# Top-32 attention into an ELU feed-forward: thresholds of both rows in one operation, and every second gate on GpSimd in the first nine blocks

## The chip, the core and the metric

The kernel runs on one core of a Trainium2 chip. The core has five engines, each with its own instruction queue worked in order: TensorE (PE in the profile, its weight loads PEld), VectorE (DVE), ScalarE (ACT), GpSimd (POOL) and SyncE (SP), which here only issues DMAs. The metric is device time in microseconds (us) of one execution, the median over several.

## The reference

Two stages follow each other. The first is attention in which each query keeps only its 32 largest scores; the second is a feed-forward layer with an ELU between its two matrices.

```python
# q, k, v: (8, 8, 576, 64)
scores = scale * np.matmul(q, k.transpose(0, 1, 3, 2))
kth = np.partition(scores, -32, axis=-1)[..., -32:-31]
scores = np.where(scores >= kth, scores, -1000000000.0)
scores = scores - np.max(scores, axis=-1, keepdims=True)
attn = np.exp(scores)
attn = attn / (np.sum(attn, axis=-1, keepdims=True) + 1e-09)
x = np.matmul(attn, v)               # then (B, H, S, D) -> (B*S, H*D) = (4608, 512)
h = x @ w_in                         # w_in (512, 2048)
g = np.where(h > 0.0, h, np.exp(np.minimum(h, 0.0)) - 1.0)
out = g @ w_out                      # w_out (2048, 512)
```

The two weight matrices arrive as 64-bit floats and are turned into 32-bit floats on the chip.

## The kernel before

**Attention in steps.** The work is cut into 144 steps. A step is one tile of 128 queries and one pair of heads, so two rows of scores (i = 0 and 1) of 576 columns each. Its stations are spread over later steps of the main loop. In iteration n:

- `scores` computes the scores of step n+2 (PE, then a copy by ScalarE).
- `select` finds the 32nd largest value in both rows of step n on VectorE: four MAX8, each giving the next eight values, with three MATCH_REPLACE8 between them that blank what was found. The first eight values go to `u.first`, the last eight to `u.last`. `select` is a generator that stops four times, which cuts the iteration into quarters.
- `mask` (step n-1) turns the scores into masked exponentials, in place. With `low` the 32nd largest and `top` the largest value, GpSimd computes `neg = -low` (L368) and `gap = low - top` (L370) on 128x1 tiles, and ScalarE computes a Prelu with bias `neg` and a huge negative slope (L371), then an Exp with bias `gap` that also sums its row into `den` (L372). Row 0 is masked in the second quarter, row 1 in the third.
- `normalise` (step n-1) inverts the sums on GpSimd (L382 to L387, small operations) and scales both rows (L389, 128x576). It comes ahead of the last quarter's feed.
- `turn` (step n-2) transposes the weights on PE (L408) and copies them by ScalarE (L409); `attend` multiplies them with v (L434) and ScalarE copies the result into the block's `xT` (L461).

The first eight iterations (`n < tight`) have a loop of their own, in which the instructions' order is left to the compiler's scheduler and the weights are decoded (`hook`: L170 to L172 on ScalarE, L173 on GpSimd, L180 and L183 on VectorE, L187 on GpSimd). From the ninth on, the order on PE, ScalarE, VectorE and GpSimd is the order in which the program writes the instructions.

**Feed-forward in blocks.** Tokens are gathered in 19 blocks of one, two or three slots of 128 tokens. Blocks 0 to 4 have one slot, blocks 5 to 8 two, and then each group of four blocks has 2, 2, 3 and 2. A block has 16 `hidden` pieces and four `project` pieces for each slot. `feed`, called at each quarter of an iteration, issues as many pieces as its plan says are due.

A `hidden(f)` piece multiplies `xT` by a column strip of `w_in` on PE (L502, two PSUM buffers). ScalarE then writes the negative part into a scratch tile `n` (L510) and the positive part into `gT` (L511). After each second piece it takes the exponential of both `n` at once (L513); the scratch tile has two buffers, so it is written again two pairs later. `project` multiplies `gT` by `w_out` (L523) and sends the result out.

**The gates.** What is left of the ELU, `gT = gT + (n - 1)`, is the gate: one operation on VectorE for each pair of `hidden` pieces, eight for each block, over 256, 512 or 768 columns (L478). A pair puts its gate into the list `gates` with the quarter in which it was issued; `close_gates`, called by `feed` with keep = 2, issues those that are two quarters old, and `hidden` and `project` force out those that they need.

Of the kernel before, what the change touches and what calls it, by code (L numbers as in the profile page):

```python
# [8 lines left out]
AF = mybir.ActivationFunctionType  # L9
ALU = mybir.AluOpType  # L10
FP32 = mybir.dt.float32
# [12 lines left out]
class Tile:  # L24
# [6 lines left out]
    def __init__(self, b, qt, rows, block, cols):  # L31
        self.b, self.qt, self.rem = b, qt, qt == 4
        self.rows = rows
        self.block = block
        self.cols = cols
        self.ql = cols.stop - cols.start
# [21 lines left out]
class Step:  # L58
# [7 lines left out]
    def __init__(self, t, hp, group, at):  # L66
        self.t, self.hp = t, hp
        self.group, self.at = group, at
        self.masked = self.normal = self.turned = False
        if t.rem:  # L70
            rows = [(4 * hp, 0), (4 * hp + 2, 0), (4 * hp + 3, 1), (4 * hp + 1, 1)]
            self.heads = [
                (h, i, slice(64 * (n % 2), 64 * (n % 2) + 64))
                for n, (h, i) in enumerate(rows)
            ]
        else:
            self.heads = [(2 * hp + i, i, slice(0, 128)) for i in range(2)]
# [3 lines left out]
def kernel(  # L81
# [9 lines left out]
    nc = tc.nc  # L91
    P = nc.NUM_PARTITIONS
# [16 lines left out]
    def pool(name, bufs, **kw):  # L109
        return ctx.enter_context(tc.tile_pool(name=name, bufs=bufs, **kw))  # L110
# [7 lines left out]
    small = pool("small", 4)  # L118
# [75 lines left out]
    def hook():  # L194

        if not decode:
            return
        decode.pop(0)()
        if not decode:
            raws.close()  # L200
            late["f"] = ctx.enter_context(tc.tile_pool(name="f", bufs=2))
            late["g"] = ctx.enter_context(tc.tile_pool(name="g", bufs=2))
            late["x"] = ctx.enter_context(tc.tile_pool(name="xt", bufs=2))
# [79 lines left out]
    def turn_qk(whole=False):  # L283
        while turning:
            if next(turning[0], turning) is turning:
                turning.pop(0)
            elif not whole:
                return
# [3 lines left out]
    def scores(u):  # L292

        u.sc = scpool.tile([P, 2, S], FP32, tag="sc", name="sc")
        q0 = QUERIES + u.t.qt * P
        for half in range(2):
            for h, i, rows in u.heads:
                kq = kqT[u.t.b, h // 2]
                part = slice(i * D, (i + 1) * D)
                k0 = (KEYS if i == 0 else 0) + half * HS  # L300
                nc.tensor.matmul(  # L301
                    wide[i][rows, half, 0:HS],
                    kq[part, q0 : q0 + u.t.ql],
                    kq[part, k0 : k0 + HS],
                    start=True,
                    stop=True,
                )
        for i in range(2):
            nc.scalar.activation(  # L309
                u.sc[:, i, :].rearrange("p (a s) -> p a s", a=2),  # L310
                wide[i][:, :, 0:HS], AF.Copy, scale=scale,
            )

    def select_row(u, i):
        if i == 0:
            u.first = small.tile([P, 2, 8], FP32, tag="m1", name="m1")
            u.last = small.tile([P, 2, 8], FP32, tag="m4", name="m4")
        sc = u.sc[:, i, :]
        m = u.first[:, i, :]
        nc.vector.max(m, sc)  # L320
        wk = wkpool.tile([P, S], FP32, tag=f"wk{i}", name="wk")
        cur = sc
        for r in range(TOP_K // 8 - 1):
            nc.vector.match_replace(wk[:], m, cur, TAKEN)
            cur = wk[:]
            if r < TOP_K // 8 - 2:
                m = small.tile([P, 8], FP32, tag=f"m{i}", name="m")[:]
            else:
                m = u.last[:, i, :]
            nc.vector.max(m, cur)  # L330
            if r == 2 or u.t.qt > 0:
                hook()
            if r != 1:
                yield

    def select(u):

        u.first = small.tile([P, 2, 8], FP32, tag="m1", name="m1")
        u.last = small.tile([P, 2, 8], FP32, tag="m4", name="m4")
        cur = [u.sc[:, i, :] for i in range(2)]  # L340
        found = [u.first[:, i, :] for i in range(2)]
        for i in range(2):
            nc.vector.max(found[i], cur[i])  # L343
        yield
        wk = [wkpool.tile([P, S], FP32, tag=f"wk{i}", name="wk")[:] for i in range(2)]
        for r in range(TOP_K // 8 - 1):
            for i in range(2):
                nc.vector.match_replace(wk[i], found[i], cur[i], TAKEN)  # L348
            cur = wk
            for i in range(2):  # L350
                if r < TOP_K // 8 - 2:
                    found[i] = small.tile([P, 8], FP32, tag=f"m{i}", name="m")[:]
                else:
                    found[i] = u.last[:, i, :]
                nc.vector.max(found[i], cur[i])  # L355
            hook()
            yield

    def mask(u, i):

        if u.masked:
            return
        if i == 0:
            u.den = small.tile([P, 2], FP32, tag="den", name="den")
        u.masked = i == 1
        sc, low, top = u.sc[:, i, :], u.last[:, i, 7:8], u.first[:, i, 0:1]
        neg = small.tile([P, 1], FP32, tag="neg", name="neg")
        nc.gpsimd.tensor_scalar_mul(neg[:], low, -1.0)  # L368
        gap = small.tile([P, 1], FP32, tag="gap", name="gap")
        nc.gpsimd.tensor_tensor(gap[:], low, top, ALU.subtract)  # L370
        nc.scalar.activation(sc, sc, AF.Prelu, bias=neg[:], alpha=STEEP)  # L371
        nc.scalar.activation(  # L372
            sc, sc, AF.Exp, bias=gap[:], accum_out=u.den[:, i : i + 1]
        )

    def normalise(u):
# [92 lines left out]
    def close_gates(keep=0, upto=None):  # L469

        while gates:
            put, group, dst, n = gates[0]
            if put > place[0] - keep if upto is None else group > upto:
                return
            gates.pop(0)
            nc.vector.scalar_tensor_tensor(  # L478
                out=dst, in0=n, scalar=-1.0, in1=dst, op0=ALU.add, op1=ALU.add
            )  # L480
# [70 lines left out]
    blocks, tight = [], 2 * NHP  # L551
    for b in range(B):
# [12 lines left out]
        for qt in range(J + 1):  # L565
            r0 = b * S + (JP if qt == J else qt)
            if qt == J:
                (blk, slot), c0, n = slots[rest], (b % 2) * R, R
                rows = slice(r0, r0 + R)
            else:  # L570
                (blk, slot), c0, n = slots[(b % 2) * J + qt], 0, P
                rows = slice(r0, r0 + J * (P - 1) + 1, J)
# [8 lines left out]
        for qts in order:  # L581
            for hp in range(NHP // 2 if qts == (J,) else NHP):
                group = Group([tiles[qt] for qt in qts], hp)
                steps += [Step(tiles[qt], hp, group, i) for i, qt in enumerate(qts)]
            for qt in qts:
                n = len(steps)
# [59 lines left out]
    def step(n):  # L646
        return steps[n] if 0 <= n < NS else None
# [3 lines left out]
    for n in range(NS + 3):  # L651
        for fn, args in todo.pop(n, []):
            fn(*args)
        ahead, cur, prev, done = step(n + 2), step(n), step(n - 1), step(n - 2)
        if n < tight:
            turn_qk(True)
            scores(ahead)
            for i in range(2):
                passes = select_row(cur, i)
                next(passes)  # L660
                if i == 0:
                    while closing:
                        attend(closing.pop(0))
                elif prev:
                    normalise(prev)
                    turn(prev, main)
                    turn(prev, rest)
                    turn(prev, other)
                feed(n, 0.25)
                next(passes)  # L670
                mask(cur, i)
                feed(n, 0.25)
            continue
        if n == tight:
            ctx.enter_context(tc.manual_schedule(engines=engines))
        passes = select(cur) if cur else iter(range(4))
        if ahead:
            scores(ahead)
        while closing:
            attend(closing.pop(0))  # L680
        next(passes)
        feed(n, 0.25)
        if prev:
            mask(prev, 0)
        turn_qk()
        next(passes)
        feed(n, 0.25)
        if done:
            turn(done, main)
            turn(done, rest)  # L690
        if prev:
            mask(prev, 1)
        next(passes)
        feed(n, 0.25)
        if done:
            turn(done, other)
        next(passes)
        if prev:
            normalise(prev)
        feed(n, 0.25)  # L700
        turn_qk(True)
# [36 lines left out]
```

## Time and profile before

| | |
|---|---|
| median of 3 runs | 1682.49 us (1682.45 to 1682.61) |
| the profiled execution | 1682.55 us, span 1680.8 us |
| PE busy | 1604.5 us (95%) |
| VectorE busy | 1534.4 us (91%) |
| ScalarE busy | 1167.5 us (69%) |
| GpSimd busy | 638.8 us (38%) |
| gates on VectorE (L478) | 152, 106.5 us |
| thresholds on GpSimd (L368, L370) | 288 and 288, 73.5 and 61.1 us |

The span is the time between the first and the last instruction that the hardware profiler recorded in one execution; the execution's own time is 1.75 us longer. All busy times are from that execution. The busy time of PE counts the matmuls from start to modelled end, so a busy PE isn't PE at its peak. Matmul records can be missing by a few per cent.

### The profile page before, as it was taken

Reading aid. Unit: us, or ns where it says so; the run is one execution under the profiler, and the core shown is the slowest. Engines: PE = TensorE matmul, PEld = TensorE weight load, DVE = VectorE, ACT = ScalarE, POOL = GpSimd, SP = SyncE. Lnnn points to the kernel's source line nnn. Section 1 sums busy time; section 2 is a strip of 40 time slices with the busy share of each in tenths; the row PEclk is TensorE's granted clock in tenths of the full one; section 3 lists DMA queues with packets and bytes.
Section 4 is the critical chain, followed back from the end, with each engine's and each line's share of the span. In section 5 each row is a group of like instructions: output and inputs, shape, how many; then the busy total and the mean of one; then the engine's idle time right before and its main releaser. Section 6 shows DMA issues by size and latency. Waiting matters only on the chain.

```text
span 1680.8 us, 26396 instructions
## 1 busy us (share of the span) xinstructions
PE 1604.5 (95%) x8560; PEld 1041.7 (62%) x8560; DVE 1534.4 (91%) x3096; ACT 1167.5 (69%) x2661; POOL 638.8 (38%) x1719
## 2 busy tenths in 40 slices
PE   6767999999999999999999999999999999999999
PEld 4554776667575666656557575756558575755565
DVE  6999999999999999999999999999998999998600
ACT  6776786778776776767768685857758586857531
POOL 3776333433333334434334333333333333332200
PEclk8567999999999999999999999999999999999999
DMA  7441021001200111001200111001100000000000
GB/s 192 134 156 39 16 56 36 7 1 47 52 7 7 29 35 42 1 21 36 49 14 1 36 35 42 1 13 43 43 13 8 21 21 29 7 7 7 7 13 13
DMA packets 101129, 56.22 MB, mean 33 GB/s; under 512 B 84097, under 2 KB 92289, under 8 KB 100993
## 3 DMA queue, kind: packets, MB, share of 16 engines
q1 hardware_dynamic: 99792, 54.26, 11.6%
q8 instruction: 68, 1.11, 0.3%
q14 instruction: 69, 0.56, 0.1%
q10 hardware_dynamic: 1200, 0.30, 0.1%
HBM read 45.09 MB, written 9.44 MB: 32 GB/s over the span
## 4 chain that ended last, share of the span: by engine, by line
PE 59%; DVE 26%; ACT 5%; issue 1%; POOL 1%; ACTq 0%; DVEq 0%; POOLq 0%
PE ops L523 22%; PE hps L502 19%; DVE wk L348 11%; DVE m L355 9%; PE avps L434 7%; PE scps L301 6%; PE eps L408 4%; DVE m L343 3%; DVE gT L478 2%; ACT sc L372 1%; ACT sc L371 1%; PE qkps L271 1%; ACT et L409 1%; PE scps L408 1%; ACT n L510 0%
## 5 line engine op out<-in xcount | busy, mean ns | idle before, releaser
L502 PE MATMUL hps<-xT,w_in 128*128 128x256 f32 (+2 forms) x2432 | 557.4, 378 | 25.9 <-ACT gT L511 23.6
L355 DVE MAX8 m<-wk 128x8 f32<-128x576 f32 x816 | 574.5, 744 | 0.0
L523 PE MATMUL ops<-w_out,gT 128*128 128x512 f32 x1152 | 523.8, 599 | 0.0
L502 PEld LDWEIGHTS hps<-xT,w_in 128*128 128x128 f32 x2432 | 411.5, 195 | 127.4 <-ACT gT L511 34.4
L348 DVE MATCH_REPLACE8 wk<-m,wk 128x576 f32<-128x576 f32 x544 | 399.2, 740 | 0.0
L523 PEld LDWEIGHTS ops<-w_out,gT 128*128 128x128 f32 x1152 | 209.0, 190 | 233.6 <-issue 218.7
L382 POOL TENSOR_SCALAR dene<-den 128x2 f32<-128x2 f32 x144 | 34.8, 242 | 832.9 <-ACT sc L372 832.7
L371 ACT ACTIVATE sc<-sc,neg 128x576 f32<-128x576 f32 x288 | 226.4, 786 | 63.2 <-POOL neg L368 63.0
L372 ACT ACTIVATE sc<-sc,gap 128x576 f32<-128x576 f32 x288 | 223.2, 775 | 25.2
L309 ACT ACTIVATE sc<-scps 128x576 f32<-128x576 f32 x288 | 173.6, 662 | 76.6 <-PE scps L301 76.6
L389 POOL TENSOR_SCALAR sc<-sc,rec 128x576 f32<-128x576 f32 x288 | 219.5, 773 | 15.2 <-POOL rec L387 0.6
L409 ACT COPY et<-eps 128x512 f32<-128x512 f32 x288 | 167.5, 582 | 68.4 <-PE eps L408 68.2
L301 PE MATMUL scps<-kqT 64*128 64x288 f32 (+1 forms) x1280 | 200.5, 439 | 15.1 <-ACT kqT L277 8.3
L348 DVE MATCH_REPLACE8 wk<-m,sc 128x576 f32<-128x576 f32 x272 | 199.6, 740 | 0.0
L408 PEld LDWEIGHTS eps<-ident,sc 128*128 128x128 f32 x1152 | 145.1, 145 | 82.9 <-issue 48.0
L478 DVE SCALAR_TENSOR_TENSOR gT<-n,gT 128x512 f32<-128x512 f32 (+2 forms) x152 | 106.5, 701 | 97.7 <-ACT n L513 97.6
L434 PE MATMUL avps<-et,vT 128*64 128x256 f32 (+2 forms) x2080 | 190.4, 326 | 2.7 <-ACT et L409 2.3
L343 DVE MAX8 m<-sc 128x8 f32<-128x576 f32 x272 | 191.0, 742 | 0.0
L408 PE MATMUL eps<-ident,sc 128*128 128x128 f32 x1152 | 178.1, 281 | 12.9 <-POOL sc L389 11.9
L510 ACT ACTIVATE n<-hps 128x256 f32<-128x256 f32 (+2 forms) x304 | 112.6, 370 | 85.5 <-PE hps L502 75.0
L434 PEld LDWEIGHTS avps<-et,vT 128*64 128x64 f32 x2080 | 123.5, 141 | 73.1 <-issue 24.2
L301 PEld LDWEIGHTS scps<-kqT 64*128 64x128 f32 (+1 forms) x1280 | 107.7, 181 | 83.6 <-issue 44.8
(47 smaller groups left out, 1226.8 us busy)
## 6 DMA issues: line engine op xcount, KB each, us to landing
kin<-in_k_dram SPq DMA_DIRECT2D x64, 128.0 KB, 2.8
raw<-in_moe_w_in_dram SPq DMA_DIRECT2D x16, 512.0 KB, 4.4
vT<-in_v_dram SPq DMA_DIRECT2D x64, 128.0 KB, 2.3
raw<-in_moe_w_out_dram SPq DMA_DIRECT2D x16, 512.0 KB, 3.2
out_dram<-osb SPq DMA_DIRECT2D x32, 256.0 KB, 2.3
qin<-in_q_dram SPq DMA_DIRECT2D x62, 128.0 KB, 2.8
kin<-in_k_dram SPq DMA_DIRECT2D x32, 32.0 KB, 2.5
vT<-in_v_dram SPq DMA_DIRECT2D x64, 16.0 KB, 2.2
```

The costliest lines, as they stand in the source:

```text
L301: nc.tensor.matmul(wide[i][rows, half, 0:HS], kq[part, q0 : q0 + u.t.ql], kq[part, k0 : k0 + HS], start=True, stop=True,)
L343: nc.vector.max(found[i], cur[i])
L348: nc.vector.match_replace(wk[i], found[i], cur[i], TAKEN)
L355: nc.vector.max(found[i], cur[i])
L371: nc.scalar.activation(sc, sc, AF.Prelu, bias=neg[:], alpha=STEEP)
L372: nc.scalar.activation(sc, sc, AF.Exp, bias=gap[:], accum_out=u.den[:, i : i + 1])
L389: nc.gpsimd.tensor_scalar(u.sc[:, i, :], u.sc[:, i, :], rec[:, i : i + 1], 1.0, ALU.mult, ALU.mult)
L408: nc.tensor.transpose(ps[:, c * P : (c + 1) * P], sc[:, c0 : c0 + P], ident[:])
L409: nc.scalar.copy(g.et[:, chunks, u.at, :], ps[:, 0 : n * P].rearrange("p (c q) -> p c q", c=n),)
L434: nc.tensor.matmul(ps[i * D : (i + 1) * D, cols], vt[:, 2 * J + i if c == J else i * J + c, :], w, start=(c == 0), stop=(c == J),)
L502: nc.tensor.matmul(ps[:, 0:n_tok], w_in[:, i, f * P : (f + 1) * P], blk.xT[:, i, 0:n_tok], start=(i == 0), stop=(i == NC - 1),)
L523: nc.tensor.matmul(blk.o[:], blk.gT[f // NG][:, f % NG, s * P : (s + 1) * P], w_out[:, f, :], start=(f == 0), stop=(f == NF - 1),)
```

## The change

The diff does two things.

*Thresholds.* A new function `bounds` computes `neg` and `gap` for a range of rows on 128x2 tiles. From the ninth iteration on it is called once a step, for both rows, at the head of the iteration (behind that iteration's loads, ahead of `scores`), where before each row had its own pair of operations inside `mask`. In the first eight iterations it is called once for each row, right ahead of `mask`.

*Gates.* `close_gates` sends some gates to GpSimd: those of blocks 0 to 8 (the first half of 19, rounded down) whose first piece f has f % 4 == 2, which is every second gate. There the gate is two operations: `n = n - 1` in place, then `gT = gT + n`.

```diff
+    def bounds(u, rows):
+
+        if u.neg is None:
+            u.neg = small.tile([P, 2], FP32, tag="neg", name="neg")
+            u.gap = small.tile([P, 2], FP32, tag="gap", name="gap")
+            u.den = small.tile([P, 2], FP32, tag="den", name="den")
+        low, top = u.last[:, rows, 7], u.first[:, rows, 0]
+        nc.gpsimd.tensor_scalar_mul(u.neg[:, rows], low, -1.0)
+        nc.gpsimd.tensor_tensor(u.gap[:, rows], low, top, ALU.subtract)
+
     def mask(u, i):
 
         if u.masked:
             return
-        if i == 0:
-            u.den = small.tile([P, 2], FP32, tag="den", name="den")
         u.masked = i == 1
-        sc, low, top = u.sc[:, i, :], u.last[:, i, 7:8], u.first[:, i, 0:1]
-        neg = small.tile([P, 1], FP32, tag="neg", name="neg")
-        nc.gpsimd.tensor_scalar_mul(neg[:], low, -1.0)
-        gap = small.tile([P, 1], FP32, tag="gap", name="gap")
-        nc.gpsimd.tensor_tensor(gap[:], low, top, ALU.subtract)
+        sc, neg, gap = u.sc[:, i, :], u.neg[:, i : i + 1], u.gap[:, i : i + 1]
         nc.scalar.activation(sc, sc, AF.Prelu, bias=neg[:], alpha=STEEP)
         nc.scalar.activation(
-            sc, sc, AF.Exp, bias=gap[:], accum_out=u.den[:, i : i + 1]
+            sc, sc, AF.Exp, bias=gap, accum_out=u.den[:, i : i + 1]
         )
...
             gates.pop(0)
+            if group[0] < len(blocks) // 2 and group[1] % 4 == 2:
+                nc.gpsimd.tensor_scalar_add(n, n, -1.0)
+                nc.gpsimd.tensor_tensor(dst, dst, n, ALU.add)
+                continue
             nc.vector.scalar_tensor_tensor(
                 out=dst, in0=n, scalar=-1.0, in1=dst, op0=ALU.add, op1=ALU.add
             )
...
                 feed(n, 0.25)
                 next(passes)
+                bounds(cur, slice(i, i + 1))
                 mask(cur, i)
                 feed(n, 0.25)
             continue
         if n == tight:
             ctx.enter_context(tc.manual_schedule(engines=engines))
         passes = select(cur) if cur else iter(range(4))
+        if prev and prev.neg is None:
+            bounds(prev, slice(0, 2))
         if ahead:
             scores(ahead)
```

More of the change, by code (lines that the diff above doesn't have):

```diff
@@ L69, in __init__ @@
         self.masked = self.normal = self.turned = False
+        self.neg = None
         if t.rem:
```

## The prediction

> **What bounds the kernel now.** I read the page's busy slices first, then busy time by stretches of the span, then the chain of waits, then the waits of the engines that the change touches.
>
> ```profile
> PE 1604.5 (95%) x8560; PEld 1041.7 (62%) x8560; DVE 1534.4 (91%) x3096; ACT 1167.5 (69%) x2661; POOL 638.8 (38%) x1719
> ...
> 50.00:156.00 106.00, 77.19 (x357) 54.99 (x353) 100.21 (x174) 82.12 (x186) 76.33 (x108) 0.68 0.36 119
> 156.00:282.50 126.50, 113.42 (x880) 82.62 (x880) 125.68 (x263) 90.16 (x238) 47.08 (x137) 0.97 0.14 35
> 282.50:365.00 82.50, 76.62 (x559) 55.46 (x560) 81.90 (x176) 63.08 (x175) 32.78 (x97) 1.00 0.01 4
> 365.00:717.00 352.00, 346.87 (x1920) 232.60 (x1918) 351.34 (x720) 261.61 (x594) 137.57 (x397) 1.00 0.10 26
> 717.00:1590.00 873.00, 869.44 (x4423) 542.49 (x4422) 833.20 (x1685) 615.10 (x1353) 321.79 (x923) 1.00 0.08 22
> ```
>
> The first line is the whole span (busy time per engine). The others are stretches, with the busy time of PE, PEld, DVE, ACT and POOL in that order, then PE's granted clock, the DMA share and GB/s. Two engines are nearly full and hand over to each other. From 717 to 1590 PE has 3.6 us idle in 873, and DVE 40. From 365 to 717 DVE has 0.7 us idle and PE 5.1. Before 282 PE has holes and POOL is busiest while the weights are decoded (76 of 106 us).
>
> ```profile
> 282.77 0.31 ACT n L513
> 283.08 0.02 issue
> 283.10 0.42 DVE gT L478
> 283.53 1.46 DVE wk L348 x3
> ...
> 711.96 0.68 DVE m L355
> 712.98 0.78 ACT sc L371
> ...
> 717.59 2.37 PE avps L434 x18
> 719.96 3.63 PE ops L523 x8
> ```
>
> This is the chain of work that ended last (start, us, what). It says where a gate's time counts. At 283 it passes from ACT to DVE: a gate had to wait for its exponential. From there to 712 it runs almost only on DVE, gates included, and from 717 to the end it is PE. From 156 to 282 it alternates between PE and ACT, without DVE; at about 135 to 156 it is decode work on DVE and POOL. So DVE time removed between 283 and 717 can shorten the run, but only by as much as PE has slack there; DVE time removed elsewhere mostly becomes idle time.
>
> **The change: what leaves DVE.** Blocks 0 to 8 have eight gates each, and the second, fourth, sixth and eighth leave: 36 in all. By the gate's rows that is half of 5.51 us before 156, of 7.05 from 156 to 282, of 6.46 from 282 to 365, and of 22.60 from 365 to 717: 2.8, 3.5, 3.2 and 11.3, together 20.8 us.
>
> **What they cost on GpSimd.** No row shows this pair of operations. The one-input half is near L389 (0.75 us for 576 columns) and L386 (0.20 us for 2): 0.96 ns a column, so 0.44 us for 256 columns and 0.69 for 512. For the add, the nearest row is the integer add L187, 1.29 us for 512; with the 0.21 us of L385 for 2 columns that gives 0.75 for 256. A gate is then 1.19 us (twenty of 256 columns) or 1.98 us (sixteen of 512): 55.5 us of POOL. From below, an add as quick as a one-input pass makes it 38; from above, twice the integer row makes it about 91. I take 55.5, the row of the same shape. The thresholds give back POOL time: L368 and L370 cost 0.255 and 0.212 us, and from the ninth step on two of the four disappear, 136 x 0.47 = 64 us over the run.
>
> **Is POOL's part hidden?** POOL works in order, so the question is where the gates stand in its queue.
>
> ```profile
> POOL dene L382 <- ACT sc L372: 186.4, 34, 8.3
> POOL neg L368 <- DVE m L355: 8.9, 17, 1.7
> ```
>
> These are POOL's waits from 365 to 717 (us in total, times, longest). Once per step POOL sits 5.5 us waiting for ScalarE's exponential sum before it can normalise. From the steps of the two-slot blocks (5 to 8) on, the moved gates are closed in the first or second quarter of a step, so they follow the thresholds and precede that wait: 2 us into a hole of 4.4 us or more. The next reader of the same scratch n is the block's hidden pair after next. Comparing its start with the time POOL would be done, fourteen of the sixteen are in time, and two (blocks 6 and 8, second gate) are about 0.5 us late. Cost 0 to 1 us; if the hole were not there, 2 us a gate, 32 us.
>
> The thresholds now wait for both rows' last MAX8, 0.74 us later than row 0 alone. Behind them on POOL wait that step's gates and normalise; ScalarE's mask waits for them. In the steps where POOL waits for DVE at all, ScalarE still has scores or relus to do before the mask, and in the others the thresholds are held by the previous normalise, as before. I cost this at nothing; uncovered it would be 0.74 us x 17 = 13 us. They are moved ahead of the first quarter's gates on POOL only; the DMA queue and the program order of PE and ScalarE past the first eight steps stay.
>
> The one-slot blocks are tighter: a hidden pair takes some 3 us and a scratch n is rewritten two pairs later.
>
> ```profile
> 187.31 0.44 ACT L513 ACTIVATE n<-n 128x256 f32<-128x256 f32 x1
> ...
> 188.23 1.64 POOL L389 TENSOR_SCALAR sc<-sc,rec 128x576 f32<-128x576 f32 x2
> 188.79 0.45 DVE L478 SCALAR_TENSOR_TENSOR gT<-n,gT 128x256 f32<-128x256 f32 x1
> 189.34 0.28 ACT L510 ACTIVATE n<-hps 128x128 f32<-128x128 f32 x1 [1.59 <-DVE gT L478]
> ```
>
> Block 1's fourth gate ran on DVE at 188.8 and ScalarE was already waiting for it. On POOL it stands behind the normalise that ends at 189.9, so it ends at about 191.1 to 191.6: ScalarE, and then PE, stand 2 us more, in the stretch where they are the chain. The other gates of blocks 1 to 4, placed the same way, end before their deadline or within 0.3 us of it. I count +1.5 us for 156 to 282 (0 to 4).
>
> **A rule against the change.** A gate reads two tensors, and in the trace such a DVE operation does not run beside GpSimd:
>
> ```profile
> 122.34 1.29 POOL L187 TENSOR_TENSOR w_out<-raw 128x512 int32<-128x512 int32 x1 [0.94 <-DVE raw L183]
> 122.85 1.06 DVE L478 SCALAR_TENSOR_TENSOR gT<-n,gT 128x256 f32<-128x256 f32 x1
> ```
>
> This gate is 0.40 us elsewhere; here it ended only after POOL's add did. MAX8 and MATCH_REPLACE8 stay at 0.74 us beside the same adds. So POOL's new gates can hold up only the other DVE gates and the decode's DVE operations. The 36 gates left on DVE mostly come in a step's third and fourth quarters, away from POOL's, so I count 0.5 us; if every one met an add of 1.29 us it would be 46. The Trainium skill ("GPSIMD Engine Reference", section 4.1, Engine selection) says to put elementwise work on VectorE, GpSimd being about twice as slow on two inputs; by that rule alone the 20.8 us come back as some 42, a loss of 21 if POOL set the pace. The trace has POOL 38% busy, so here the rule prices the wrong engine.
>
> **The sum.** Before 156: DVE gives up 2.8 us, two of the four gates lying on the chain, and POOL, at 72% busy there, gets 4.8 us and the decode behind it: 0, between -3 and +4. From 156 to 282: +1.5. From 282 to 365: 3.2 us leave the chain and PE has 5.9 us idle to take them up; I take -2.7, as PE there also waits for ScalarE's relus. From 365 to 717: 11.3 us leave the chain, but PE allows less. It idles 5.1 us and keeps 0.4% idle even where it is the bound (1.4 us), so 3.7; pacing the matmuls' starts at their mean intervals of 1000 to 1500 gives some 7. I take -5. After 717 PE is the bound and nothing changes. Sum -6.2 us. The profiled execution was 1682.55 us (span 1680.8 and 1.75 around it), 0.06 from the median 1682.49, so the forecast is 1676.3 us. A measurement can tell 0.2%, 3.4 us, from no change.
>
> **The rivals.**
> *PE takes over at once.* The DVE time goes, but PE's idle time is latency that stays, and ScalarE's new waits eat the rest: -2.7 - 1.5 + 1.5 + 1 = about -2, 1681 us. For it: PE over 98% busy from 365 on. Against: after 717 PE shows that it can run at 99.6%. Chance 0.15.
> *GpSimd becomes the bound of the early stages; slower.* Place: the decode and blocks 0 to 4, to 365. If each of those twenty gates holds up the decode, a mask or a scratch buffer for one gate's 1.2 us, that is 24 us; with half of them 12, less 5 us of gain later: +7, about 1690. It decides once a gate regularly ends after the relu that rewrites its scratch. For it: POOL at 72% and shared access in the decode, and the waiting relu above. Against: only one of sixteen gates in blocks 1 to 4 is clearly late. Chance 0.22.
> *Everything is taken up.* 3.2 + 7, and 3 in the decode where DVE operations stretch to over 1 us, with nothing lost: -13, 1669.5. Chance 0.13, because it needs every cover to hold.
>
> **How the numbers follow.** The forecast has 0.50 (inside 1672 to 1679). The range of 1669 to 1689 takes in the full gain and nearly all of the slower rival's mean, leaving out 2 in 10. Faster by over 0.2%: forecast and full gain, 0.63. Within: 0.15. Slower: 0.22.
>
> **What would show it.** Right: the chain turns to PE long before 717, at some 400 to 500; DVE shows idle time waiting for ScalarE from 282 on; PE idle from 365 on falls towards 0.4%; POOL's wait for the exponential shrinks by the gates' time without ScalarE waiting longer for neg; the point where the weights are decoded stays near 156. Wrong: ScalarE's relu into n waits for POOL by over 5 us in total, the decode ends some us later, or POOL's gate takes far over 2 us.

## The result, and the profile after

The changed kernel takes 1687.88 us (median of 6, 1686.62 to 1688.53) against 1682.55 for the kernel before beside it: 5.3 us more, a ratio of 1.0031 with a 95% interval of 1.0019 to 1.0043. The forecast was 6.2 us less. The profiled execution has a span of 1685.7 us.

Line numbers are those of each kernel, so the same operation can have another one after the change; the names of the tiles stay. Busy time of the engines in that execution, then the same stretches as before (start and end, length, busy time of PE, PEld, DVE, ACT and POOL, PE's granted clock, DMA share, GB/s):

```profile
PE 1603.5 (95%) x8560; PEld 1038.7 (62%) x8560; DVE 1518.2 (90%) x3060; ACT 1167.8 (69%) x2661; POOL 662.0 (39%) x1519
...
50.00:156.00 106.00, 75.21 (x337) 54.78 (x338) 96.50 (x165) 82.38 (x186) 82.37 (x116) 0.69 0.38 121
156.00:282.50 126.50, 112.93 (x867) 81.05 (x866) 123.73 (x258) 86.27 (x228) 55.90 (x130) 0.99 0.13 32
282.50:365.00 82.50, 75.09 (x563) 55.42 (x562) 79.68 (x169) 62.34 (x175) 39.75 (x92) 1.00 0.03 9
365.00:717.00 352.00, 346.78 (x1914) 230.52 (x1913) 343.18 (x704) 261.80 (x594) 167.22 (x364) 1.00 0.10 26
717.00:1590.00 873.00, 869.92 (x4420) 541.65 (x4419) 833.71 (x1687) 617.87 (x1357) 291.82 (x756) 1.00 0.08 22
```

VectorE did get its time back: from 365 to 717 it now idles 8.8 us, where it idled 0.7. PE did not: 5.2 us idle there, as against 5.1. The chain that ended last agrees; its first line, the shares of the span by engine:

```profile
PE 80%; ACT 9%; DVE 4%; POOL 4%; issue 2%; SPq 1%; DMA 1%; ACTq 0%; POOLq 0%
```

Before, the same line was:

```profile
PE 59%; DVE 26%; ACT 5%; issue 1%; POOL 1%; ACTq 0%; DVEq 0%; POOLq 0%
```

The chain moved from VectorE to PE, and the end did not come sooner.

Where the 5 us arose is read by comparing the starts of the matmuls with the same number (counted from the first) in the two traces. At 95 us of the kernel before the changed one is 0.2 us late, at 135 it is 3.2, at 185 2.6, at 200 3.9, at 365 4.3, at 717 5.4 and at 1590 4.9. So 3 us are lost in the weight decode, 1.3 within a few us of 191, and 1.5 in small jumps from 200 to 717; little of it is regained.

The price of a gate is in the groups of the changed kernel (busy us, mean ns; L485 is the subtraction of 1, L486 the add):

```profile
L485 POOL TENSOR_SCALAR n<-n 128x512 f32<-128x512 f32 x16 | 24.1, 1505 | 0.0
...
L486 POOL TENSOR_TENSOR gT<-gT,n 128x512 f32<-128x512 f32 x16 | 20.4, 1278 | 1.3
...
L485 POOL TENSOR_SCALAR n<-n 128x256 f32<-128x256 f32 x20 | 17.5, 876 | 9.3 <-ACT n L523 9.3
...
L486 POOL TENSOR_TENSOR gT<-gT,n 128x256 f32<-128x256 f32 x20 | 15.0, 750 | 1.5
```

The add costs what was counted (1.28 and 0.75 us); the subtraction costs twice as much, 1.50 and 0.88 us instead of 0.69 and 0.44. A gate of 512 columns thus takes 2.78 us on GpSimd, where the usual one on VectorE takes 0.67. In all the gates take 77.0 us of GpSimd, not 55.5.

### The profile page after: what moved, and what is told of

Same layout as the page of the kernel before. It is cut to its first block, busy times and chain, and to the rows that moved or that the text cites. A ratio compares the mean times of both kernels' runs of the same rounds, so it can differ in the third digit from the quotient of the medians.

```text
span 1685.7 us, 26028 instructions
## 1 busy us (share of the span) xinstructions
PE 1603.5 (95%) x8560; PEld 1038.7 (62%) x8560; DVE 1518.2 (90%) x3060; ACT 1167.8 (69%) x2661; POOL 662.0 (39%) x1519
## 4 chain that ended last, share of the span: by engine, by line
PE 80%; ACT 9%; DVE 4%; POOL 4%; issue 2%; SPq 1%; DMA 1%; ACTq 0%; POOLq 0%
PE ops L533 29%; PE hps L512 25%; PE avps L439 9%; PE scps L302 8%; PE eps L413 6%; ACT sc L377 2%; ACT sc L376 2%; PE qkps L272 1%; ACT et L414 1%; DVE wk L349 1%; ACT n L520 1%; DMA raw<-in_moe_w_in_dram 1%; POOL raw L174 1%; PE scps L413 1%; POOL sc L394 1%
## 5 line engine op out<-in xcount | busy, mean ns | idle before, releaser
L302 PE MATMUL scps<-kqT 64*128 64x288 f32 (+1 forms) x1280 | 197.3, 436 | 17.8 <-ACT kqT L278 8.1
L439 PE MATMUL avps<-et,vT 128*64 128x256 f32 (+2 forms) x2080 | 189.8, 325 | 2.3 <-ACT et L414 2.0
L488 DVE SCALAR_TENSOR_TENSOR gT<-n,gT 128x512 f32<-128x512 f32 (+2 forms) x116 | 86.9, 750 | 114.3 <-ACT n L523 114.3
L439 PEld LDWEIGHTS avps<-et,vT 128*64 128x64 f32 x2080 | 120.1, 140 | 75.0 <-issue 24.1
L302 PEld LDWEIGHTS scps<-kqT 64*128 64x128 f32 (+1 forms) x1280 | 106.0, 180 | 85.5 <-issue 44.1
```

Of the source, the lines that this page charges most:

```text
L302: nc.tensor.matmul(wide[i][rows, half, 0:HS], kq[part, q0 : q0 + u.t.ql], kq[part, k0 : k0 + HS], start=True, stop=True,)
L439: nc.tensor.matmul(ps[i * D : (i + 1) * D, cols], vt[:, 2 * J + i if c == J else i * J + c, :], w, start=(c == 0), stop=(c == J),)
```

## The experiments

Theory A: PE sets the pace from 282 us on, so freed VectorE time is worth nothing, and the loss sits at a few places where gates went to GpSimd. Theory B: the later threshold of row 0 delays ScalarE's masks all along the run. Rival C: the freed time is worth the 5 us or so that were forecast, and GpSimd's gates eat it all along the run. Each figure is against the kernel before on the same chip.

### The thresholds alone

```diff
-            if group[0] < len(blocks) // 2 and group[1] % 4 == 2:
-                nc.gpsimd.tensor_scalar_add(n, n, -1.0)
-                nc.gpsimd.tensor_tensor(dst, dst, n, ALU.add)
-                continue
```

> Only the thresholds' part of the change; all gates stay on VectorE. Theory A (the loss sits at a few places where gates went to GpSimd: block 0's gates inside the weight decode, about +3.2 us, and block 1's fourth gate, about +1.3; the thresholds cost nothing, and the freed VectorE time is worth nothing because PE already sets the pace from 282 us on): within 0.5 us of before. Theory B (the later threshold of row 0 delays ScalarE's masks all along the run): +3 us or more, with PE falling behind steadily from the ninth step to 1590.

Measured: 1681.59 us against 1682.85, ratio 0.9992 (0.9983 to 1.0001). Not slower: theory B falls. A second comparison gave the same size:

> The kernel with the thresholds' part alone once more, as the candidate that could beat both: -0.5 to -1.5 us to before if the first comparison (-1.3) was real, within 0.5 us if it was chance.

Measured: 1681.30 against 1682.66, 0.9994 (0.9985 to 1.0003). That is -1.3 and -1.4 us, but each interval takes in 1.

### Without block 0, and block 0 alone

```diff
-            if group[0] < len(blocks) // 2 and group[1] % 4 == 2:
+            if 1 <= group[0] < len(blocks) // 2 and group[1] % 4 == 2:
```

> The whole change, but block 0's four gates stay on VectorE; PE's and ScalarE's program order is then that of before. Theory A: about +2 us to before, the matmuls level with before until 190 us. Rival C (freed VectorE time is worth some 5 us, and what eats it is GpSimd's gates all over blocks 1 to 8): still about +5 us, or, if block 0 was what ate it, below before by 2 us or more.

Measured: 1684.51 against 1682.85, 1.0009 (1.0000 to 1.0018): +1.7 us.

```diff
+            if group[0] == 0 and group[1] % 4 == 2:
```

> Thresholds as changed, and only block 0's four gates on GpSimd; PE's and ScalarE's program order is that of the changed kernel, which differs from before in two spots during the decode. Theory A: +3 us to before, reached by 132 us and constant from there on. Rival C: near 0.

Measured: 1684.07, 1.0006 (0.9998 to 1.0015). That is +1.2 to before and +2.5 to the thresholds alone, which ran on the same chip; by the matmuls' starts +2.9 at 135 us. Here is what the first of the four does. GpSimd's operations and their waits around 100 us, first before, then in the changed kernel:

```profile
98.66 0.61 POOL L173 TENSOR_SCALAR raw<-raw 128x512 f32<-128x512 f32 x1 [0.85 <-ACT raw L170]
...
100.35 1.47 POOL L187 TENSOR_TENSOR w_out<-raw 128x512 int32<-128x512 int32 x1
...
101.90 0.53 POOL L368 TENSOR_SCALAR neg<-m 128x1 f32<-128x1 f32 x1
...
102.47 0.78 ACT L371 ACTIVATE sc<-sc,neg 128x576 f32<-128x576 f32 x1 [0.63 <-POOL neg L368]
```

```profile
98.22 0.88 POOL L485 TENSOR_SCALAR n<-n 128x256 f32<-128x256 f32 x1 [1.66 <-ACT n L523]
...
99.19 0.73 POOL L486 TENSOR_TENSOR gT<-gT,n 128x256 f32<-128x256 f32 x1
...
100.00 0.61 POOL L174 TENSOR_SCALAR raw<-raw 128x512 f32<-128x512 f32 x1
...
100.65 1.52 DVE L181 TENSOR_SCALAR raw<-raw 128x512 uint32<-128x512 uint32 x1 [0.81 <-POOL raw L174]
...
103.97 0.55 POOL L367 TENSOR_SCALAR neg<-m 128x1 f32<-128x1 f32 x1
...
104.55 0.78 ACT L376 ACTIVATE sc<-sc,neg 128x576 f32<-128x576 f32 x1 [2.57 <-POOL neg L367]
```

GpSimd waits 1.66 us for the exponential, works 1.6 us on the gate, and the decode and the mask behind it come 2 us late; VectorE and ScalarE now wait for GpSimd. The scheduler also orders a few of PE's and ScalarE's instructions differently when these gates are on GpSimd. Time or order was told apart by shrinking the gates and leaving the order of PE, ScalarE and VectorE:

```diff
+            if group[0] == 0 and group[1] % 4 == 2:
+                n, dst = n[:, :, 0:1], dst[:, :, 0:1]
```

> As the run with block 0's gates only on GpSimd, but those four gates work on the first column of each half only (the rest of these gates is left out). The order on PE and ScalarE stays that of the changed kernel, GpSimd keeps both operations and their waits, but they shrink from some 0.45 and 0.75 us to 0.2 each. If the decode's loss is GpSimd's time: +0.5 to +1.5 us to before. If it is the scheduler's other order (or the waits of the queue): still +3 us.

Measured: 1681.40, 0.9990 (0.9981 to 0.9999): the level of the thresholds alone, below what was expected. The order on PE, ScalarE and VectorE and GpSimd's waits for the exponential (1.66 us at the first gate here, too) cost nothing; it is GpSimd's time, 2.7 us of loss for the 7.0 us of work in four gates, of which 1.9 stay here. GpSimd's own order did not quite stay: at three spots neighbouring decode operations, thresholds and gate operations stand the other way round, and this run does not tell that from the time. The run with a cheaper subtraction further down does: there the order is that of the changed kernel on all four engines, the four gates are 2.3 us shorter, and by the matmuls' starts the loss at 135 us falls from 3.2 to 2.0.

### Is freed VectorE time worth anything?

```diff
-            if group[0] < len(blocks) // 2 and group[1] % 4 == 2:
+            if 5 <= group[0] < len(blocks) // 2 and group[1] % 4 == 2:
```

> Thresholds as changed, and only the sixteen gates of blocks 5 to 8 (the two-slot blocks, 365 to 717 us) on GpSimd: 11.3 us leave VectorE where the prediction counted -5. Theory A (PE sets the pace there, its idle time is latency that stays): within 1.3 us of before, more likely above it. Rival C (the relief is real and was eaten elsewhere): -3 to -5 us.

Measured: 1683.04 against 1682.64, 1.0001 (0.9992 to 1.0010).

On the kernel before, ahead of the gate on VectorE:

```diff
+            if 5 <= group[0] < len(blocks) // 2 and group[1] % 4 == 2:
+                continue
```

> The kernel before, with the second, fourth, sixth and eighth gate of blocks 5 to 8 left out altogether (their part of the ELU is missing from the output): the relief of VectorE without any cost on GpSimd. Theory A: within 0.7 us of before. Rival C: -4 us or more; that would leave GpSimd's part as what eats it.

Measured: 1682.36, 0.9998 (0.9989 to 1.0007). Half the gates of four blocks gone, at no cost on GpSimd, and the time stands still. Rival C falls for 365 to 717.

On the kernel before, behind the gate on VectorE:

```diff
+            if 5 <= group[0] < len(blocks) // 2 and group[1] % 4 == 2:
+                nc.vector.scalar_tensor_tensor(
+                    out=n, in0=n, scalar=-1.0, in1=n, op0=ALU.add, op1=ALU.max
+                )
```

> The kernel before, with a second operation of the same size on VectorE behind each of those sixteen gates (into the scratch tile, which is no longer read): 11.3 us more on VectorE from 365 to 717. If VectorE set the pace there, as the chain of waits said: +11 us, and its mirror image with the gates left out should gain. Theory A, with PE as the bound and VectorE exactly as full: a loss of less than 11 us, by what its backlog of up to two steps does not absorb; I expect +5 to +9.

Measured: 1693.87 against 1682.64, 1.0066 (1.0053 to 1.0079): +11.2 us, all of what was added; I had expected a part to be absorbed. The loss does not come gradually: by the matmuls' starts PE loses nothing until 511 us, by when six of the sixteen extra operations have run, then about 6.6 us from 511 to 536 and 4.7 from 693 to 697. So 11 us more on VectorE cost their full length and 11 us less gain nothing: its work and PE's in these 352 us are matched. PE's idle time shows what ends its waits. All that PE waited for from 365 to 717, before, with those gates left out, and with VectorE burdened (us in total, times, longest):

```profile
PE scps L259 <- ACT sc L309: 3.9, 4, 1.2
PE avps L434 <- ACT et L409: 0.9, 2, 0.6
PE eps L408 <- ACT kqT L277: 0.3, 1, 0.3
```

```profile
PE scps L259 <- ACT sc L309: 3.9, 4, 1.2
PE avps L434 <- ACT et L409: 0.9, 2, 0.6
PE eps L408 <- ACT kqT L277: 0.6, 1, 0.6
```

```profile
PE hps L506 <- ACT gT L515: 5.5, 2, 2.7
PE scps L259 <- ACT sc L309: 3.9, 4, 1.2
...
PE avps L434 <- ACT et L409: 0.9, 2, 0.6
```

The 5.1 us idle of PE are four transposes of k that wait until ScalarE has copied the scores out of a shared PSUM tile, and some smaller waits of the same kind. VectorE ended none of it, and with those gates left out the same waits stand. With VectorE burdened, a new wait appears in front of them: the relus, held up by late gates.

From 282 to 365, where eight more gates left VectorE, no run left them out. PE's longest wait there, before and in the changed kernel, is:

```profile
PE hps L502 <- ACT gT L511: 6.1, 9, 1.3
```

```profile
PE hps L512 <- ACT gT L521: 6.6, 10, 1.3
```

ScalarE ended it in both. That the relief is worth nothing there, too, is argued from these lines, not shown by a run.

### The late gates

In the kernel without block 0, block 1's fourth gate looks as the prediction drew it:

```profile
187.46 1.48 POOL L394 TENSOR_SCALAR sc<-sc,rec 128x576 f32<-128x576 f32 x2
...
188.90 0.87 POOL L485 TENSOR_SCALAR n<-n 128x256 f32<-128x256 f32 x1
...
189.86 0.73 POOL L486 TENSOR_TENSOR gT<-gT,n 128x256 f32<-128x256 f32 x1
...
190.62 0.28 ACT L520 ACTIVATE n<-hps 128x128 f32<-128x128 f32 x1 [3.75 <-POOL gT L486]
```

It stands behind the scaling of the previous step, and ScalarE's next relu into that scratch waits 3.75 us for it.

```diff
-            if 1 <= group[0] < len(blocks) // 2 and group[1] % 4 == 2:
+            if 1 <= group[0] < len(blocks) // 2 and group[1] % 4 == 2 and group != (1, 6):
```

> As the run with the gates of blocks 1 to 8 on GpSimd, but block 1's fourth gate, the one the prediction called late, stays on VectorE: 31 gates on GpSimd. Theory A: 1.3 us less than with that gate on GpSimd, so about +0.7 us to before. Rival: that gate is one of many, and the time changes by 0.3 us or less.

Measured: 1682.88 against 1682.64, 1.0001 (0.9992 to 1.0010): +0.2 instead of +1.7. One gate of 32 made nearly all of it. The length of a wait is not its price, though. In this run, too, ScalarE's relu waits as long for another gate, block 4's sixth:

```profile
356.83 0.28 ACT L520 ACTIVATE n<-hps 128x128 f32<-128x128 f32 x1 [3.76 <-POOL gT L486]
```

By the matmuls' starts PE falls only some 0.4 us further behind from 330 to 365: during most of that wait it had scores (L302, 1.24 us) and a group of matmuls with v (L439, 2.38 us) to do. At block 1's fourth gate, in the run from block 1 on, it fell 1.6 us behind.

The same for the two that the prediction called late in blocks 6 and 8:

```diff
+            if 5 <= group[0] < len(blocks) // 2 and group[1] % 4 == 2 and group not in ((6, 2), (8, 2)):
```

> Thresholds as changed and the gates of blocks 5 to 8 on GpSimd, except the second gates of blocks 6 and 8, which the prediction called late by 0.5 us. Theory A: the 1.4 us that these sixteen gates cost over the thresholds alone fall to 0.5 or less, so -0.8 us or lower to before. Rival: the cost is spread over the sixteen, and at least 1 us of it stays.

Measured: 1680.76 against 1682.66, 0.9988 (0.9979 to 0.9997): -1.9 us, as against +0.4 with these two on GpSimd. The other fourteen cost nothing that can be measured. It was run again:

> The version with the gates of blocks 5 to 8 on GpSimd in the form of the change, except the second of blocks 6 and 8, once more: -1 to -2 us to before if the first comparison (-1.9) was real.

Measured: 1680.74 against 1682.55, 0.9990 (0.9981 to 0.9999).

### The price of the subtraction

```diff
-                nc.gpsimd.tensor_scalar_add(n, n, -1.0)
+                nc.gpsimd.tensor_scalar(n, n, -1.0, 0.0, ALU.add, ALU.add)
```

> The changed kernel, with the gate's first operation on GpSimd written with two steps (add -1, add 0) like the scaling in normalise, instead of one. In the changed kernel the one-step form took 1.50 us for 512 columns and 0.88 for 256, where the two-step scaling takes 0.75 for 576. If the form sets the price: about 0.7 us for 512 columns, a gate ends 0.4 to 0.8 us sooner, and the loss of 5 us shrinks by 1.5 to 3. If it is the tile (three-dimensional, in place): still 1.5 us, no change in time.

Measured: 1689.39 against 1682.66, 1.0038 (1.0025 to 1.0050): +6.7 us. Neither alternative: the subtraction became slower, 1.94 us for 512 columns. With block 0's gates on VectorE:

> The same two-step form, with block 0's gates left on VectorE. With the one-step form this was +1.7 us to before. If lateness of a few gates is the whole loss of blocks 1 to 8: 0 to +0.8 us. It cannot be clearly below the run with thresholds alone (-1.3), because PE sets the pace.

Measured: 1686.41, 1.0022 (1.0013 to 1.0031): +3.8 us, where the one-step form had +1.7. A miss, too, but it shows how steeply the time rises with a gate's price. So the forms were laid side by side behind the end of the kernel before:

> The kernel before, with nine forms of a one-input operation over 512 columns on GpSimd behind its end, four times each, in place on a scratch tile. If the kind of operation sets the price: the add about 1.5 us in both shapes, (add, add) about 1.9, the forms that only multiply about 0.7. If the number of steps or a scalar read from memory does: one-step forms 1.5, and only (multiply, multiply) with a scalar from memory 0.7. If the shape does: 128x2x256 slow and 128x512 fast.

The groups of those nine lines in one execution (512 columns each; busy us, mean ns):

```profile
L715 POOL TENSOR_SCALAR n<-n 128x512 f32<-128x512 f32 x4 | 7.7, 1934 | 0.3
L716 POOL TENSOR_SCALAR n<-n 128x512 f32<-128x512 f32 x4 | 6.0, 1511 | 0.3
L713 POOL TENSOR_SCALAR n<-n 128x512 f32<-128x512 f32 x4 | 6.0, 1501 | 0.2
L714 POOL TENSOR_SCALAR n<-n 128x512 f32<-128x512 f32 x4 | 6.0, 1492 | 0.3
L718 POOL TENSOR_SCALAR n<-n 128x512 f32<-128x512 f32 x4 | 2.8, 695 | 0.4
L717 POOL TENSOR_SCALAR n<-n 128x512 f32<-128x512 f32 x4 | 2.5, 620 | 0.3
L719 POOL TENSOR_SCALAR n<-n 128x512 f32<-128x512 f32 x4 | 2.5, 620 | 0.3
L720 POOL TENSOR_SCALAR n<-n 128x512 f32<-128x512 f32 x4 | 2.5, 620 | 0.3
L721 POOL TENSOR_SCALAR n<-n 128x512 f32<-128x512 f32 x4 | 2.5, 614 | 0.3
```

L713 is the add in the gate's shape (128x2x256), L714 the add in 128x512, L715 (add, add), L716 a single multiply, L717 (multiply, multiply), L718 the same with a scalar from memory, L719 (multiply, add), L720 that in the gate's shape, L721 (min, max). Shape does not matter for the two forms that ran in both. Two-step forms that begin with a multiply or a min take 0.61 to 0.70 us; one-step forms 1.5, the multiply too; (add, add) 1.9. None of my three explanations holds alone; why the pairs are quick was not found.

```diff
-                nc.gpsimd.tensor_scalar_add(n, n, -1.0)
+                nc.gpsimd.tensor_scalar(n, n, 1.0, -1.0, ALU.mult, ALU.add)
```

> The changed kernel, with the gate's first operation written as (multiply by 1, add -1). If this form runs at 0.7 us for 512 columns: a gate ends 0.4 to 0.8 us sooner than in the changed kernel, and of its loss of 5 us some 1.5 to 3 go. If it costs as much as (add, add): +6 to +7 us to before.

Measured: 1682.81 against 1682.01, 1.0005 (0.9996 to 1.0014): +0.8 us instead of +5.3, with the subtraction at 0.62 and 0.42 us. At the counted price the change is about neutral.

### What is left

```diff
+            if 1 <= group[0] < len(blocks) // 2 and group[1] % 4 == 2 and group != (1, 6):
+                nc.gpsimd.tensor_scalar(n, n, 1.0, -1.0, ALU.mult, ALU.add)
...
-        nc.gpsimd.tensor_scalar_mul(u.neg[:, rows], low, -1.0)
+        nc.gpsimd.tensor_scalar(u.neg[:, rows], low, -1.0, 0.0, ALU.mult, ALU.add)
```

> Thresholds as changed, with the negation in the two-step form (multiply, add); the second, fourth, sixth and eighth gates of blocks 1 to 8 on GpSimd in the form (multiply 1, add -1), except block 1's fourth. If nothing but price and lateness cost time, and the relief of VectorE is worth nothing: the same as thresholds alone, -1 to -2 us to before. If the relief is worth something after all: -3 us or more.

Measured: 1680.29 against 1682.55, 0.9986 (0.9977 to 0.9995): -2.3 us. It beats both kernels, and so does the version with fourteen gates. Neither can be told from the thresholds alone (-1.3 and -1.4): the gates on GpSimd at best cost nothing.

## Why the prediction was wrong, step by step

**365 to 717: -5 us counted, about +1 measured.** This is the step that failed first. The prediction saw 5.1 us of idle PE, saw the chain of waits run on VectorE, and took VectorE to be what PE idled for. It did not ask what had ended that idle time; the waits of PE in that window, above, name ScalarE for all of it. The chain was misread too: it follows VectorE because VectorE is never idle there, not because its time was the price. Leaving the gates out (-0.3 us) shows the forecast gain was not there to be had. The rival "PE takes over at once" had this mechanism, with 1681 us, and against it I set PE's 99.6% after 717. But there the same k transposes make up 2.4 of PE's 3.6 idle us; they only wait more seldom, three times in 873 us as against four in 352.

**282 to 365: -2.7 counted, +0.8 in the traces.** In all likelihood the same error; I noted that PE waits there for ScalarE's relus and still credited most of the relief. The loss fits two gates that the prediction had within 0.3 us of their deadline: in the changed kernel ScalarE's relu waited 1.37 us for block 3's fourth and 3.76 for block 4's sixth. They were not tested one by one.

With these two credits at nothing the prediction's sum is +1.5 us, and the run whose gates cost about what was counted measured +0.8. That this comes so close is partly luck: the decode lost 2.0 us there by the matmuls' starts at 135 us, where nothing was counted, and the thresholds gave some 1.3 that were not counted either.

**Decode: 0 counted, +2.5 to +3 measured.** Within the stated -3 to +4, but the value taken was wrong. GpSimd's queue was counted as having room at 72% busy, but decode and masks stand behind each gate, and its time delays them; the gates' wait for the exponential, with the gates shrunk, cost nothing. The slower rival named this place and this mechanism, and its 1690 us is near the 1687.9 measured, but by luck: it had half of the twenty early gates late by a gate's time, 12 us, and 5 us of later gain. The sixteen gates of blocks 1 to 4 cost 1.3 us together (+1.7 with blocks 1 to 8, +0.4 with 5 to 8), nearly all of it one gate, and the gain was not there.

**156 to 282: +1.5 counted, +0.5 net in the traces, with +1.3 at one gate.** Right in place and mechanism: block 1's fourth gate, 1.4 us by the times of the runs with and without it, 1.6 by the matmuls' starts. The two gates called late in blocks 6 and 8 were late, too, at 2.3 us for the pair instead of 0 to 1.

**A gate's price: 55.5 us counted, 77.0 measured**, inside the bounds of 38 (from the rows named it comes to 40) and 91. The add was right; the subtraction was priced by two-step rows (L389, L386), and the change uses the one-step form. There was a hint in small, though none of the size: L368, a one-step multiply of one column, took 0.255 us where the two-step L386 took 0.199 for two. This term is the difference between +5.3 and +0.8 us: it lengthens the decode and pushes gates over their deadlines.

**Thresholds: nothing counted, -1.3 and -1.4 us measured**, not clear of zero. The later threshold for row 0 costs nothing, as argued.

**The rule against the change.** The prediction's reading that a gate does not run beside GpSimd is too wide. In the changed kernel gates on VectorE took their usual 0.40 and 0.69 us beside the new subtraction (at 98.8 and 494.9 us), but 1.05 to 1.12 beside a decode add and up to 1.21 beside the scaling of both rows. The 36 gates that stayed on VectorE took 22.9 us instead of 20.8, where 0.5 us more were counted. GpSimd's add took what the row before suggested, 1.28 us for 512 columns, against 0.67 for VectorE's whole gate. The page's factor of two on two-input operations (GPSIMD Engine Reference in the Trainium skill, section 4.1, Engine selection) is about what this case shows, 1.9; the loss came where the extra time met a deadline, not in proportion to it.

**The signs.** All three signs of being wrong came: ScalarE's relu waited 8.0 us for GpSimd's gates, the decode ended 3 us later, and a gate took 2.78 us. But of the signs of being right some came as well: the chain turned to PE at 411 us, long before 717, VectorE idled 8.8 us from 365 to 717, and GpSimd's wait for the exponential there shrank from 186.4 to 167.3 us. They show that VectorE was relieved, not that the end comes sooner. The one that bears on the time, PE's idle time falling, did not come (5.2 us, as against 5.1).

## What to carry to other kernels

Two engines that are both full can be matched: before counting what relief of one is worth, ask what ended the other's idle time, in that stage, and leave the work out once to see whether the time moves. A chain of waits that stays on an engine without idle time shows that it has no time to spare (here 11.3 us more cost 11.2), not that less work on it ends sooner. Work moved to an engine with spare time costs little as long as it ends before its reader's deadline and holds up nothing behind it, so check each instance against its place in the in-order queue and price the operation by the row of its exact form.

## What the runs showed of the hardware that was not expected

On GpSimd the form of a one-input operation over 512 columns of 32-bit floats decides its time by a factor of three: 0.62 us for (multiply, add), (multiply, multiply) and (min, max), 1.50 us for a single add or multiply, 1.93 us for (add, add). The single add, (multiply, add) and (add, add) took the same in both tile shapes, 128x512 and 128x2x256.
